# One activation table set, work moved to GpSimd, a table of due times and reordered transposes in a gated linear attention with two expert layers

## The chip, the cores and the metric

The kernel runs on one core of a Trainium2 chip. The metric is the device time of one execution in microseconds; of several executions the median is given. The profile is one profiled execution, and its times count from the span's start.

## The reference

A gated linear attention over 4 batches, 8 heads, 768 steps and a head size of 48 feeds two dense layers on 3072 tokens. All data are float32.

```python
f = 1.0 / (1.0 + np.exp(-f_logit))
for t in range(S):
    state = f[:, :, t, :, None] * state + np.einsum('bhd,bhe->bhde', k[:, :, t], v[:, :, t])
    y[:, :, t] = np.einsum('bhd,bhde->bhe', q[:, :, t], state)
# y -> x: 3072 tokens x 384
h = x @ w_in                                   # 384 x 2048
g = np.where(h >= 1, h, np.where(h <= -1, 0, (h + 1) ** 2 / 4))
x = g @ w_out                                  # 2048 x 384
gate = x @ w_gate; val = x @ w_val             # 384 x 1536 each
out = (gate / (1 + np.exp(-gate)) * val) @ w_out2   # 1536 x 384
```

The gates' logits are scaled by eight after they are drawn.

## The kernel before

**Tiles.** The attention is cut into 24 units: unit u holds 128 steps of batch u % 4, all heads, in two chunks c of 64 steps. The layers run over six groups of 512 tokens; a group is four units. A pass is one layer over one group; `PASSES` orders the twelve: first layer groups 0 and 1, second layer 0 and 1, and so on. The first layer needs the output of the group's four units, so units 0 to 3 come ahead of everything and units 4 to 7 during pass 0; units 8 to 23 are worked in two groups of eight, during the second layer's passes.

**A unit.** ScalarE and VectorE make the running products of the gates and their inverses (tiles e, x). For units 0 to 3 that is done with logarithms: `log_ops` (L496 to L503) takes exp, VectorE a minimum, ScalarE ln; a matmul sums (`at_cum`, tile psc), and two exponentials follow (L520, L526). For the others `decay_ops` (L532) takes exp and sigmoid, VectorE adds one (L548, L553) and scans (L559, L567). VectorE multiplies k (L574) and q (L584). TensorE makes the scores (psa, L606), transposes k (pst, L614), updates the state (psu, L670) and makes the output (psy, L699). ScalarE copies pst to kn. The mask is VectorE's (L632) or, for units from 4 on, ScalarE's copy and GpSimd's select. `at_state` adds psu to the state (L680) and multiplies it by the chunk's decay (L682), both on VectorE; `at_state_out` (L690) copies the state on GpSimd into vs or vf, which psy reads. In `at_burst` a visit of units 8 to 23 is made of up to three parts: psu of one unit, psa and pst of the next, and psy of the one before, which is an operation of its own.

**Precision.** An expert product is three matmuls: the high part of a float32 number times the high part, and the two cross terms. `c_b`, `c_sh`, `c_or`, `c_sg`, `c_h`, `c_l` make the weights' two parts from 64-bit input, each pair of blocks once; pairs go to DRAM and are loaded from there in later passes. `g_hi` and `g_lo` (L802, tile gl, the remainder) split what lies between two products.

**Zeroing.** Parts of vs, vf and y and the scans' tables d1 and dr must hold constants; they are written at L317 to L331, L475, L476 and L713.

**Order.** A planner writes the order of all engines' work. Every operation is added with an engine, a duration, its dependencies, a due time (`prio`) and buffers that it takes and gives; the planner steps through them, and among those of an engine that can start soon takes the one that is due first. So each engine's queue, SP's queue of DMA issues among them, has an order fixed at build time. An operation with a `tab` other than the last one costs 1.28 us in the plan. While TensorE would wait, ahead of the first expert products, the planner puts in filler matmuls (tile wt, L839), the planned gap divided by `FQ` in number.

## Time and profile before

| what | us |
|---|---|
| median of 3 runs | 958.18 (957.96 to 959.22) |
| profiled execution | 956.27 |
| its span | 954.5 |
| TensorE (matmul) busy | 935.5 |
| VectorE busy | 544.8 |
| ScalarE busy | 466.6 |
| GpSimd busy | 153.7 |

PE is TensorE, PEld its weight loads, DVE VectorE, ACT ScalarE, POOL GpSimd, and SP the engine that issues DMAs. L-numbers are lines of the kernel before. A stage table gives the engines in the order PE, PEld, DVE, ACT, POOL, and where one line is asked for, that line's engine alone. An engine counts as busy from the start of an instruction to its end. TensorE's instructions overlap, so its busy time is not a measure of its pace.

### The profile page before, as it was taken

How to read it: one execution, taken by the hardware profiler on the slowest of the kernel's cores; microseconds unless marked ns; L12 is line 12 of the kernel's file. 1: busy time of each engine (PE TensorE's matmuls, PEld its weight loads, DVE VectorE, ACT ScalarE, POOL GpSimd, SP SyncE). 2: the span in 40 equal slices, each digit the busy share in tenths (PEclk: the TensorE clock that was granted, in tenths of full speed). 3: DMA queues.
4: the chain of work that ended last, by engine and by line, in shares of the span. 5: the costliest groups of instructions: out<-in, count | busy, mean ns of one | idle time of the engine just before them, and what ended most of it. 6: DMA issues, size and time to landing. Idle time of an engine off the chain costs nothing.

```text
span 954.5 us, 15762 instructions
## 1 busy us (share of the span) xinstructions
PE 935.5 (98%) x6312; PEld 763.6 (80%) x6312; DVE 544.8 (57%) x794; ACT 466.6 (49%) x728; POOL 153.7 (16%) x256
## 2 busy tenths in 40 slices
PE   7899999999999999999999999999999999999996
PEld 7766778888888888888888888888888888888884
DVE  6999988998976565333435645664433433433332
ACT  6867766644445446545444425464654543222221
POOL 6435702113122131000000002132000000000000
PEclk9999999999999999999999999999999999999998
DMA  7936789688736872106647005576101755001001
GB/s 293 272 101 202 219 288 388 227 312 302 287 104 223 275 223 60 51 0 231 199 166 210 1 28 180 195 264 205 48 3 65 277 190 196 1 1 34 1 0 38
DMA packets 50594, 151.66 MB, mean 159 GB/s; under 512 B 5424, under 2 KB 24624, under 8 KB 50512
## 3 DMA queue, kind: packets, MB, share of 16 engines
q1 hardware_dynamic: 50512, 150.56, 46.9%
q8 instruction: 52, 0.85, 0.4%
q14 instruction: 30, 0.25, 0.1%
HBM read 110.43 MB, written 36.18 MB: 154 GB/s over the span
## 4 chain that ended last, share of the span: by engine, by line
PE 90%; DVE 3%; ACT 3%; DMA 1%; issue 1%; POOL 1%; DVEq 0%; POOLq 0%; ACTq 0%; SPq 0%
PE hp L773 19%; PE gps L773 15%; PE vps L773 15%; PE acc L425 11%; PE acc L426 11%; PE acc L427 11%; PE psy L699 2%; PE wt L839 1%; DMA raw<-w 1%; PE pst L614 1%; PE acc L811 1%; DVE raw L378 1%; DVE w L410 1%; PE psb L670 1%; PE psb L607 1%
## 5 line engine op out<-in xcount | busy, mean ns | idle before, releaser
L773 PE MATMUL hp<-xh,w 128*128 128x512 f32 x576 | 194.9, 395 | 0.3 <-DVE g L785 0.3
L425 PE MATMUL acc<-gh,w 128*128 128x512 f32 x480 | 187.2, 390 | 0.0
L426 PE MATMUL acc<-gl,w 128*128 128x512 f32 x480 | 187.0, 390 | 0.0
L427 PE MATMUL acc<-gh,w 128*128 128x512 f32 x480 | 186.8, 389 | 0.0
L773 PE MATMUL gps<-xh,w 128*128 128x512 f32 x432 | 146.5, 393 | 0.2 <-DVE sg L793 0.2
L773 PE MATMUL vps<-xh,w 128*128 128x512 f32 x432 | 144.7, 389 | 0.0
L773 PEld LDWEIGHTS hp<-xh,w 128*128 128x128 f32 x576 | 108.0, 188 | 24.5 <-issue 1.7
L785 DVE SCALAR_TENSOR_TENSOR g<-g,hp 128x512 f32<-128x512 f32 x96 | 65.7, 684 | 98.9 <-ACT g L782 98.7
L778 ACT ACTIVATE g<-hp,half 128x512 f32<-128x512 f32 x96 | 66.2, 690 | 100.6 <-PE hp L773 95.8
L773 PE MATMUL hp<-xl,w 128*128 128x512 f32 x288 | 112.0, 390 | 0.3 <-DVE xl L433 0.3
L793 DVE TENSOR_TENSOR sg<-gps,sg 128x512 f32<-128x512 f32 x72 | 49.6, 689 | 104.5 <-ACT sg L789 104.3
L797 ACT CAST gh<-sg 128x512 fp32r<-128x512 f32 x72 | 44.7, 621 | 130.2 <-DVE sg L793 130.2
L426 PEld LDWEIGHTS acc<-gl,w 128*128 128x128 f32 x480 | 90.1, 188 | 19.3 <-DVE gl L802 0.7
L425 PEld LDWEIGHTS acc<-gh,w 128*128 128x128 f32 x480 | 90.1, 188 | 18.8
L427 PEld LDWEIGHTS acc<-gh,w 128*128 128x128 f32 x480 | 90.1, 188 | 18.7
L789 ACT ACTIVATE sg<-gps 128x512 f32<-128x512 f32 x72 | 43.1, 599 | 113.7 <-PE gps L773 108.1
L773 PEld LDWEIGHTS gps<-xh,w 128*128 128x128 f32 x432 | 81.1, 188 | 17.9 <-DVE sg L793 0.7
L773 PEld LDWEIGHTS vps<-xh,w 128*128 128x128 f32 x432 | 81.1, 188 | 16.8
L802 DVE TENSOR_TENSOR gl<-g,gh 128x512 fp32r<-128x512 f32 x88 | 62.0, 704 | 47.0 <-ACT gh L797 46.8
L773 PE MATMUL gps<-xl,w 128*128 128x512 f32 x216 | 84.2, 390 | 0.0
L773 PE MATMUL vps<-xl,w 128*128 128x512 f32 x216 | 84.0, 389 | 0.0
L797 ACT CAST gh<-g 128x512 fp32r<-128x512 f32 x88 | 54.6, 620 | 57.2 <-DVE g L785 57.0
(146 smaller groups left out, 1281.3 us busy)
## 6 DMA issues: line engine op xcount, KB each, us to landing
w<-w2d SPq DMA_DIRECT2D x36, 768.0 KB, 4.3
raw<-w SPq DMA_DIRECT2D x34, 768.0 KB, 7.1
w<-w1d SPq DMA_DIRECT2D x32, 768.0 KB, 6.0
w2d<-w SPq DMA_DIRECT2D x18, 768.0 KB, 8.4
w1d<-w SPq DMA_DIRECT2D x16, 768.0 KB, 7.7
qk<-qk SPq DMA_DIRECT2D x20, 448.0 KB, 7.5
x2d<-o SPq DMA_DIRECT2D x18, 256.0 KB, 2.4
xl<-x2d SPq DMA_DIRECT2D x6, 768.0 KB, 7.9
```

Of the source, the lines that this page charges most:

```text
L378: nc.vector.scalar_tensor_tensor(out=lo, in0=hi, scalar=3, in1=lo, op0=ALU.logical_shift_left, op1=ALU.bitwise_or)
L425: nc.tensor.matmul(o, w[:, 0, wsl], xh, start=first, stop=False)
L426: nc.tensor.matmul(o, w[:, 0, wsl], xl, start=False, stop=False)
L427: nc.tensor.matmul(o, w[:, 1, wsl], xh, start=False, stop=last)
L699: nc.tensor.matmul(psy[0:48, i], vs[0:112, 0, c, p], a["ma"][0:112, i], start=True, stop=True)
L773: nc.tensor.matmul(hp, w[:, p, k * 128:(k + 1) * 128], x[:, k], start=i == 0, stop=i == len(steps) - 1)
L778: nc.scalar.activation(g, hp, AF.Relu, bias=half, scale=0.5)
L785: nc.vector.scalar_tensor_tensor(out=g, in0=g, scalar=1.0, in1=hp, op0=ALU.min, op1=ALU.max)
L789: nc.scalar.activation(sg, gps, AF.Sigmoid)
L793: nc.vector.tensor_tensor(out=sg, in0=p, in1=sg, op=ALU.mult)
L797: nc.scalar.copy(gh, g)
L802: (nc.gpsimd if pool else nc.vector).tensor_tensor(out=gl, in0=g, in1=gh.bitcast(F32), op=ALU.subtract)
```

## The change

- ScalarE loads one table set by name ahead of all; in the planner exp and ln are one `tab`, and the exponentials of units 2 and 3 no longer wait for those of unit 1.
- The zeroing of vf and of y for unit 2 is GpSimd's; d1 and dr are filled by an operation of their own on VectorE, on which the scans depend.
- For units 0 to 7 (`PST`) the multiplication by the decay becomes a planner operation on GpSimd, save the first chunk of units 0 to 3.
- For units 4 and 6 (`ADACT`) ScalarE adds the one. In pass 0 GpSimd makes the remainders of blocks 8, 10, 12 and 14 (`POOL_G`).
- In a visit psy is part of the burst and comes ahead of pst.
- `DUE` replaces the due times of 487 operations: those of units 0 to 7 with their loads (indices up to 201), the preparation of the first layer's weights (535 to 654), and pass 0 with the start of pass 1 (867 to 1044).
- Fillers: `FQ` is 0.125 instead of 0.12, and they may use a second buffer when the first is taken.
- Some durations and latencies in the planner's entries are new; the diff shows those of exp, minimum and ln, and leaves out those of loads.

```diff
--- before.py
+++ after.py
@@ -35,7 +35,7 @@
 POOL_K = ()
-POOL_G = 0
+POOL_G = (8, 10, 12, 14)
 SEL = (4, 5, 6, 7)
@@ -46,11 +46,75 @@
 EARLY2 = (3, 5, 7, 9, 11)
-FT, FQ, F0 = 60, 0.12, 4
+FT, FQ, F0 = 60, 0.125, 4
 KK = DM // 128
 BLEAD, BGAP = 34.0, 14.0
+ADACT = (4, 6)
+PST = (0, 1, 2, 3, 4, 5, 6, 7)
+DUE = {
+    0: 16.29, 1: -0.01, 2: -73.18, 3: -11.59, 4: 27.73, 5: -265.18, 6: -156.68, 7: -253.62, 8: -166.14, 9:
...
+}
 EXTRA = {0: 13.0, 2: 4.0}
@@ -75,7 +139,7 @@
         after, left, ready = {}, {}, {}
-        free, done, tab = dict(Pool=5.0, DVE=2.5), {}, None
+        free, done, tab = dict(Pool=5.0, DVE=1.8), {}, None
         for i, o in enumerate(ops):
@@ -125,13 +189,13 @@
             del ready[o["eng"]][i]
-            idle = min(self.slots["py"], default=t) <= free.get("PE", 0.0) + 0.3
+            idle = next((k for k in ("py", "pa") if min(self.slots[k], default=t) <= free.get("PE", 0.0) + 0.3), None)
             for tag in o["take"]:
             if fill and o["eng"] == "PE" and t < FT and idle:
-                fill(int((t - max(free.get("PE", 0.0), F0)) / FQ))
+                fill(int((t - max(free.get("PE", 0.0), F0)) / FQ), idle)
             o["t"] = t
@@ -291,6 +355,7 @@
+    nc.scalar.preload_act_table_set("natural_log_exp_and_others")
     x2d = dram.tile([128, KK, NT], F32, name="x2d")
@@ -314,10 +379,6 @@
     nc.gpsimd.memset(uno, 1.0)
-    nc.vector.memset(d1, 0.0)
-    nc.vector.memset(d1[:, :, 0:1], 1.0)
-    nc.vector.memset(dr, RCAP)
-    nc.vector.memset(dr[:, :, 0:1], 1.0)
     nc.vector.memset(half, 0.5)
@@ -472,8 +533,8 @@
             VF[2 + i] = t[:, i]
-            nc.vector.memset(t[0:64, i, 1], 0.0)
-            nc.vector.memset(t[64:112, i, 0], 0.0)
+            nc.gpsimd.memset(t[0:64, i, 1], 0.0)
+            nc.gpsimd.memset(t[64:112, i, 0], 0.0)
@@ -545,12 +606,12 @@
                 lambda: nc.scalar.activation(x, x, AF.Exp, scale=-1.0),
-                lambda: nc.vector.tensor_scalar(x, x, 1.0, None, op0=ALU.add),
+                lambda: nc.scalar.activation(x, x, AF.Copy, bias=1.0) if u in ADACT else nc.vector.tensor_scalar(x, x, 1.0, None, op0=ALU.add),
             ]
             lambda: nc.scalar.activation(x, x, AF.Sigmoid),
-            lambda: nc.vector.tensor_scalar(e, e, 1.0, None, op0=ALU.add),
+            lambda: nc.scalar.activation(e, e, AF.Copy, bias=1.0) if u in ADACT else nc.vector.tensor_scalar(e, e, 1.0, None, op0=ALU.add),
         ]
@@ -650,7 +711,7 @@
-    def at_burst(a, s):
+    def at_burst(a, s, y=None):
@@ -658,6 +719,9 @@
             at_psa(a, [t[:, 0:4 * C].rearrange("p (a t) -> p a t", a=4) for t in both])
+        if y:
+            at_pe3(y)
+        if a:
             at_pst(a, "h", 2)
@@ -673,13 +737,16 @@
         b = u % B
-        src = ST[b]
         if u < B and c == 0:
-            src = a["psu"][c]
-        else:
-            nc.vector.tensor_tensor(out=ST[b], in0=a["psu"][c], in1=ST[b], op=ALU.add)
-        pend = a["pp"].rearrange("p (a c) t -> p a c t", c=2)[:, :, c, C - 1:C]
-        nc.vector.tensor_tensor(out=ST[b], in0=src, in1=pend.to_broadcast([112, NP, D]), op=ALU.mult)
+            at_pend(u, c, a["psu"][c], nc.vector)
+            return
+        nc.vector.tensor_tensor(out=ST[b], in0=a["psu"][c], in1=ST[b], op=ALU.add)
+        if u not in PST:
+            at_pend(u, c, ST[b], nc.vector)
+
+    def at_pend(u, c, src, eng):
+        pend = A[u]["pp"].rearrange("p (a c) t -> p a c t", c=2)[:, :, c, C - 1:C]
+        eng.tensor_tensor(out=ST[u % B], in0=src, in1=pend.to_broadcast([112, NP, D]), op=ALU.mult)
@@ -700,6 +767,12 @@
+    def at_d():
+        nc.vector.memset(d1, 0.0)
+        nc.vector.memset(d1[:, :, 0:1], 1.0)
+        nc.vector.memset(dr, RCAP)
+        nc.vector.memset(dr[:, :, 0:1], 1.0)
+
     def at_y(u):
@@ -710,7 +783,7 @@
         if u < 4:
-            nc.vector.memset(a["y"][32:64], 0.0)
+            (nc.gpsimd if u else nc.vector).memset(a["y"][32:64], 0.0)
...
@@ -888,7 +961,7 @@
             if not odd:
-                E["y", u] = add("DVE", 1.1, lambda u=u: at_y(u), (), -44.8 + u, ("w" if u else "y",))
+                E["y", u] = add("Pool" if u else "DVE", 0.95, lambda u=u: at_y(u), (), -44.8 + u, ("w" if u else "y",))
             yc = E["yc", u] = add("ACT", 1.18, lambda u=u: at_yc(u), (p3, E["y", u // 2 * 2]), b + 4, (), ("py",))
@@ -927,11 +1000,8 @@
         pb = py = None
-        if a or c:
-            dur = 0.2 + 0.9 * (a is not None) + 0.52 * (c is not None)
-            pb = add("PE", dur, lambda: at_burst(a, c), deps, b + 1, take, give)
-        if y:
-            py = add("PE", 1.05, lambda: at_pe3(y), (pb,) if pb else deps, b + 1 - 9 * (pb is not None), () if pb else take, ("mab",))
+        dur = 0.2 + 0.9 * (a is not None) + 0.52 * (c is not None) + 0.95 * (y is not None)
+        pb = py = add("PE", dur, lambda: at_burst(a, c, y), deps, b + 1, take, give + (("mab",) if y else ()))
         mc = None
@@ -949,21 +1019,22 @@
+    E["d"] = add("DVE", 1.1, at_d, (), -20.0)
     for u in range(NU):
...
             )
...
         if u == 2:
-            E["vf"] = add("DVE", 1.7, at_vf, (), -44.5, ("w",))
+            E["vf"] = add("Pool", 1.7, at_vf, (), -44.5, ("w",))
         before = {2: E.get("vf"), 3: E.get("vf"), 4: E.get(("p3", 0)), 5: E.get(("p3", 1))}.get(u, E.get(("p3", u - 2)))
         if u < 4:
...
             E["lv", u] = add("Pool", 1.4, lambda u=u: at_copyv(u), (E["n", u], before), b + 1)
@@ -978,9 +1049,9 @@
                     bl = at_base(u // 4 * 4) - 6 + u % 4 + (i or 0)
-                    ex = add("ACT", 0.9 * h, lambda lg=lg: lg(0), (E["lx", u],) + ((E["ep", 1],) if u == 2 else ()), bl, tab="exp")
-                    mn = add("DVE", 0.9 * h, lambda lg=lg: lg(1), (ex,), bl)
-                    ln = add("ACT", 0.9 * h, lambda lg=lg: lg(2), (mn,), bl + 4, tab="ln")
+                    ex = add("ACT", 1.02 * h, lambda lg=lg: lg(0), (E["lx", u],), bl, tab="exp")
+                    mn = add("DVE", 0.75 * h, lambda lg=lg: lg(1), (ex,), bl)
+                    ln = add("ACT", 1.15 * h, lambda lg=lg: lg(2), (mn,), bl + 0.4, tab="exp")
                     for h in (0, 1) if i is None else (i,):
@@ -997,7 +1068,7 @@
                 ex, sg = sg, ex
-            ad = add("DVE", 0.72, lambda F=F: F[None][2](), (ex,), b - 2)
+            ad = add("ACT" if u in ADACT else "DVE", 1.07 if u in ADACT else 0.72, lambda F=F: F[None][2](), (ex,), b - 2)
             for i in range(2):
@@ -1005,8 +1076,8 @@
         else:
-            R = add("DVE", 1.3, lambda u=u: at_scan_r(u), (E["ad", u],), b)
-            Pp = add("DVE", 1.28, lambda u=u: at_scan_p(u), (E["sg", u],), b + 0.2)
+            R = add("DVE", 1.3, lambda u=u: at_scan_r(u), (E["ad", u], E["d"]), b)
+            Pp = add("DVE", 1.28, lambda u=u: at_scan_p(u), (E["sg", u], E["d"]), b + 0.2)
         pk = u in POOL_K
...
@@ -1041,9 +1112,14 @@
             leave(u - 1, p2)
-        s0 = add("DVE", 0.37 if u < B else 0.75, lambda u=u: at_state(u, 0), (p2, so0, E.get(("st", u - B))), b + 2.2, (), ("at",))
+        pm = u in PST
+        s0 = add("DVE", 0.37 if u < B or pm else 0.75, lambda u=u: at_state(u, 0), (p2, so0, E.get(("st", u - B))), b + 2.2, (), ("at",))
+        if pm and u >= B:
+            s0 = add("Pool", 0.7, lambda u=u: at_pend(u, 0, ST[u % B], nc.gpsimd), (s0,), b + 2.2)
         so1 = add("ACT" if u in ACT_S else "Pool", 0.72 if u in ACT_S else 0.8 if u < 4 else 1.4, lambda u=u: at_state_out(u, 1), (s0, E.get(("p3", u - 2 if u > 5 else u - 4)), E.get("vf") if u in (2, 3) else None), b + 2.2)
-        s1 = add("DVE", 0.75, lambda u=u: at_state(u, 1), (so1, E.get(("st", u - 1)) if odd else None), b + 4, (), ("at", two) if odd else ("at",))
+        s1 = add("DVE", 0.37 if pm else 0.75, lambda u=u: at_state(u, 1), (so1, E.get(("st", u - 1)) if odd else None), b + 4, (), ("at",) if pm else ("at", two) if odd else ("at",))
+        if pm:
+            s1 = add("Pool", 0.7, lambda u=u: at_pend(u, 1, ST[u % B], nc.gpsimd), (s1, E.get(("st", u - 1)) if odd else None), b + 4, (), (two,) if odd else ())
         E["st", u] = s1
...
@@ -1153,8 +1229,7 @@
                 hi = None if nat else add("ACT", 0.65, keep(("gh", key), g_hi, ("g", key)), (mx,), b + 1, ("gh",))
-                pool = s == 1 and pool_n < POOL_G and j % 2 == 0
-                pool_n += s == 1
+                pool = n == 0 and j in POOL_G
                 lo = None if nat else add(
@@ -1200,6 +1275,8 @@
         o["order"] = tuple(d for d in (takeX.get(d[1] - 1) if isinstance(d, tuple) else d for d in o["order"]) if d is not None)
+    for i, p in DUE.items():
+        P.ops[i]["prio"] = p
     with tc.manual_schedule():
```

## Rows read from the trace of the kernel before

**Rows 1.** Stage table: stretch, us, busy us per engine (instructions), granted clock, DMA, GB/s.

```profile
0.00:42.95 42.95, 35.32 (x638) 32.26 (x638) 32.53 (x68) 34.63 (x49) 23.51 (x61) 0.96 0.82 278
42.95:126.72 83.77, 81.53 (x673) 56.90 (x672) 78.49 (x107) 59.92 (x95) 43.82 (x49) 1.00 0.58 183
126.72:954.50 827.78, 818.67 (x5003) 674.41 (x5003) 433.82 (x621) 372.04 (x586) 86.42 (x146) 1.00 0.44 150
```

**Rows 2.** ScalarE in order of time: start, us, instructions, [idle before, its releaser].

```profile
3.50 1.11 ACT L500 ACTIVATE x<-x 128x448 f32<-128x448 f32 x2 [1.40 <-DMA x<-xn]
6.39 1.28 ACT L502 ACT_TABLE_LOAD   x1 [1.78 <-DVE x L501]
...
10.23 0.60 ACT L520 ACTIVATE e<-psc 112x512 f32<-112x512 f32 x1
```

**Rows 3.** The chain that ended last, from 0 to 140 us: start, duration, what.

```profile
19.66 1.28 ACT L520
...
47.33 1.54 PE wt L839 x24
...
125.71 0.96 DVE xl L433
```

**Rows 4.** VectorE in order of time, the same columns as ScalarE's.

```profile
4.02 0.38 DVE L475 MEMSET vf<- 64x384 f32 x1
...
5.92 0.69 DVE L501 TENSOR_SCALAR x<-x 128x448 f32<-128x448 f32 x2
...
10.86 0.69 DVE L574 TENSOR_TENSOR qk<-qk,e 112x512 f32<-112x512 f32 x1 [3.07 <-ACT e L520]
```

**Rows 5.** All engines in order of time, ahead of the first expert matmul.

```profile
40.00 3.02 PE L839 MATMUL wt<-btri 128*64 128x64 f32 x38
...
41.31 0.55 DVE L750 TENSOR_TENSOR xl<-px,xh 128x384 fp32r<-128x384 f32 x1
```

**Rows 6.** GpSimd in order of time.

```profile
5.12 0.41 POOL L331 MEMSET vs<- 48x384 f32 x1
9.32 1.53 POOL L489 COPY vs<-qk 64x192 f32<-64x192 f32 x4 [3.79 <-DMA qk<-vv]
```

**Rows 7.** DMA issues of SP in order of time: start, time to issue.

```profile
1.73 0.91 SPq L456 DMA_DIRECT2D qk<-qf  x2
```

**Rows 8.** The DMA issued from 1.2 to 1.9 us: KB, us to landing.

```profile
qk<-qf SPq DMA_DIRECT2D x1, 512.0 KB, 5.7
```

**Rows 9.** Line L682 alone in the first pass, stage table.

```profile
43.00:127.00 84.00, 4.58 (x8) 1.00 0.58 184
```

**Rows 10.** Groups from 43 to 127 us: count, busy us, mean ns, idle before.

```profile
L404 POOL CAST w<-raw 128x768 fp32r<-128x768 f32 (+1 forms) x13 | 13.7, 1051 | 17.6 <-DVE raw L391 14.1 <-issue 3.3
...
L690 POOL COPY vs<-st 48x192 f32<-48x192 f32 x12 | 10.5, 872 | 4.4 <-DVE st L682 3.9
...
L802 DVE TENSOR_TENSOR gl<-g,gh 128x512 fp32r<-128x512 f32 x7 | 5.3, 762 | 0.0
...
L591 POOL COPY mb<-ma 64x512 f32<-64x512 f32 x4 | 4.9, 1224 | 6.9 <-DVE ma L584 6.9
```

**Rows 11.** TensorE's waits: for whom, total us, times, longest.

```profile
PE psy L699 <- POOL vs L690: 1.0, 1, 1.0
```

**Rows 12.** Single lines: count, duration in ns min/median/max, first and last start.

```profile
L682 DVE TENSOR_TENSOR st<-st,x x40: 357/359/818, 19.0 to 673.6; 112x192 f32<-112x192 f32 x40
...
L690 POOL COPY vs<-st x84: 337/344/2087, 17.9 to 672.9; 48x192 f32<-48x192 f32 x84
```

**Rows 13.** VectorE in order of time, late in the first pass.

```profile
117.02 1.55 DVE L682 TENSOR_TENSOR st<-st,e 112x192 f32<-112x192 f32 x1
```

**Rows 14.** The chain behind visits of attention, in two stretches.

```profile
270.98 2.09 PE gps L773 x9
...
307.15 2.27 PE gps L773 x9
```

More of the change, by code (lines that the diff above doesn't have):

```diff
@@ L833, in x2_load, with fill @@
         nc.sync.dma_start(out=getX(n)[1].bitcast(F32), in_=x2d[:, :, g * 512:(g + 1) * 512])
-    def fill(n):
-        t = ps.tile([64, 64], F32, tag="acc0", name="wt")
+    def fill(n, where):
+        t = ps.tile([64, 64], F32, tag="acc0" if where == "py" else "acc1", name="wt")
         for _ in range(n):
@@ L957, in fast_path @@
             E["lx", i] = add(
-                "SP", 1.6, lambda i=i: at_loadx(i), (), b - 12 if i >= NLOG else -51.65 if i else -52.0, ("x",), (), 2.0,
+                "SP", 1.6 if i >= NLOG else 1.15, lambda i=i: at_loadx(i), (), b - 12 if i >= NLOG else -51.85 if i else -52.0, ("x",), (), 3.0 if i >= NLOG else 3.5 if i else 2.6,
                 (E.get(("l", i - 1)) if i != 2 else E["l", 0],),
             )
-        E["l", u] = add("SP", 1.75 if u < 4 else 2.1, lambda u=u: at_load(u), (), b - 11.9 if u >= 4 else -51.9 + 0.05 * u + 0.3 * (u > 1), ("w",) if u < 4 else ("qk", "vn"), (), 2.0, (E["lx", u // 2 * 2] if u != 2 else None, E.get(("l", u - 1))))
+        E["l", u] = add("SP", 2.5 if u == 0 else 1.4 if u < 4 else 2.1, lambda u=u: at_load(u), (), b - 11.9 if u >= 4 else -51.9 + 0.05 * u + 0.3 * (u > 1), ("w",) if u < 4 else ("qk", "vn"), (), 3.5 if u < 4 else 3.0, (E["lx", u // 2 * 2] if u != 2 else None, E.get(("l", u - 1))))
         if u == 2:
-            E["vf"] = add("DVE", 1.7, at_vf, (), -44.5, ("w",))
+            E["vf"] = add("Pool", 1.7, at_vf, (), -44.5, ("w",))
         before = {2: E.get("vf"), 3: E.get("vf"), 4: E.get(("p3", 0)), 5: E.get(("p3", 1))}.get(u, E.get(("p3", u - 2)))
         if u < 4:
-            E["n", u] = add("SP", 0.65, lambda u=u: at_loadn(u), (), -51.7 + 0.2 * u + 0.1 * (u > 1), (), (), 2.0, (E["l", u], E.get(("n", u - 1))))
+            E["n", u] = add("SP", 0.5, lambda u=u: at_loadn(u), (), -51.7 + 0.2 * u + 0.1 * (u > 1), (), (), 3.5, (E["l", u], E.get(("n", u - 1))))
             E["lv", u] = add("Pool", 1.4, lambda u=u: at_copyv(u), (E["n", u], before), b + 1)
@@ L1030, in fast_path @@
         if u in SEL:
-            mc = add("ACT", 1.5, lambda u=u: at_mcopy(u), (pa, qc), b + 2.4, (), ("at",) * 2 if u >= 4 else ())
+            mc = add("ACT", 1.5, lambda u=u: at_mcopy(u), (pa, qc), b + 2.4, (), ("at",) * 2 if u >= 4 else ("pa",))
             mask = add("Pool", 2.6, lambda u=u: at_msel(u), (mc,), b + 2.5)
@@ L1077, in fast_path @@
             p = use - 16
-            last_d = dma = add("SP", 2.6, lambda jb=jb: c_dma(jb), (), p - 8, (slot,), (), 2.2, (last_d,))
+            last_d = dma = add("SP", 1.95 if r == 0 and i < 4 else 2.6, lambda jb=jb: c_dma(jb), (), p - 8, (slot,), (), 3.3, (last_d,))
             cg = dma
@@ L1102, in keep @@
         return go
-    oms, pool_n, lin_at = [], 0, None
+    oms, lin_at = [], None
     for r, ns in enumerate(runs):
```

59 rows, old and new, of the table DUE are left out of this document.

## Prediction

> **What bounds the kernel now.** I read the stage table first [rows 1]. From 126.72 us to the end TensorE is busy 818.67 of 827.78 us, and what is missing there is the tail; the change can take time from that stage only by shortening TensorE's own work. The first 42.95 us hold no expert matmul at all: they are the attention of units 0 to 3, and no engine is full in them (ScalarE 34.63, VectorE 32.53, GpSimd 23.51 us busy). Between them lies the first expert pass: TensorE counts as busy for 81.53 of 83.77 us, but VectorE for 78.49, so two engines are close to the limit together, and GpSimd stands at 43.82, about half. So three stages, three questions: how much sooner can the first matmul start, can VectorE and GpSimd then keep up, and what does a visit of attention cost TensorE later on.
>
> For the front I read each engine's own order, then the chain. On ScalarE a load of a function table (1.28 us) stands ahead of each change between exp and ln: one at 6.39 ahead of the first ln, another ahead of the exp at 10.23 [rows 2]. There are four such loads before the first expert matmul, the first at 6.39, the last at 19.66, which stands itself on the chain [rows 3]. The one at 6.39 came that late because VectorE took the minimum between exp and ln only at 5.92, behind four zeroing instructions of 0.38 us from 4.02 on, though the first exponentials ran from 3.50 [rows 2, 4]. At the end of the front, xl of unit 3 is written from 41.31 on for 0.55 us, while TensorE runs 38 filler matmuls from 40.00 to the first real one at 42.95 [rows 5].
>
> **The change part by part: the front.** (a) Zeroing moved. The four vf instructions (4 x 0.38 = 1.5 us) and y of unit 2 go to GpSimd, and d1 and dr are filled later. GpSimd writes such zeros in 0.41 us and then sits idle for 3.79 us until a load lands, at 9.32 [rows 6]; the moved work is 4 x 0.41 and one y (0.95 in the planner's entry), 2.6 us in all, and lies in that gap. Were the gap gone, the copies of v would come up to 2.6 us later. VectorE can then take the minimum as soon as the first of two exponentials is done, at about 4.1 instead of 5.92: 1.8 us.
> (b) One table set. The loads at 6.39 and ahead of 10.23 go: 2 x 1.28 = 2.6 us. With (a) the exponentials of units 0 and 1 could begin 4.4 us sooner, at 5.8. But they multiply q and k, and q and k of unit 0 are issued at 1.73 and land 5.7 us later, at 7.4 [rows 7, 8]; that first multiplication stood at 10.86 [rows 4]. So the gain here is 10.86 - 7.4 = 3.4 us, and the remaining microsecond waits for memory. The other two loads (ahead of the ln of units 2 and 3, and the one at 19.66) are worth 2 x 1.28 = 2.6 us more, and the second is on the chain [rows 3]. Sum 6.0 us. The Trainium skill, "ScalarE: Activation LUTs", section "What ACT_TABLE_LOAD costs", adds a drain to the load and has a switch at 2.66 us; the rows show no drain, and by the page an estimate for four switches would be 10.6 us instead of 5.1, and the time some 5 us lower.
> (c) Fillers. TensorE could have started when xl was there, 41.86, and started at 42.95: 1.1 us [rows 5]. The divisor goes from 0.12 to 0.125, 4% fewer fillers, but filling is now also allowed where it was not; I take 0.5 us.
> (d) The due times set new priorities for the operations of units 0 to 7, of the first weights, of the first pass and of the start of the second, on all five queues, SP's loads included. They change no duration, and the trace before can't show them. Bounds: ScalarE is idle for 42.95 - 34.63 = 8.3 us of the front [rows 1], of which the first 3.50 can't go, nor all of the waits for transfers and for TensorE, so at most some 3 us; in the other direction an operation set ahead of its data blocks its queue, and the longest such wait for a load in these rows is 3.79 us [rows 6]. I take 0, between the two.
> Front: 6.0 + 0.5 = 6.5 us sooner, from 3 (little more than the step that memory bounds survives) to 9.5.
>
> **The first pass.** VectorE loses the decay multiplications of units 4 to 7, 8 in 4.58 us [rows 9]; four remainders gl, 4 x 0.76 = 3.05 [rows 10]; the additions for units 4 and 6, 0.72 each in the planner's entry. Together 9.0 us. It gains d1 and dr, 4 zeroing instructions, 1.1 us in the planner's entry. But if the front is 6.5 us shorter, the weight work that VectorE did in those 6.5 us, 6 us at its share there, has to be done later. Net it has 9.0 - 1.1 - 6 = 1.9 us less: enough to keep up, no more. What could be gained are TensorE's visible waits: 1.54 us of fillers at 47.33 [rows 3] and 1.0 us for GpSimd's state copies [rows 11]; the second pass then starts behind xl at 125.71 [rows 3]. I take 1.0 us of these 2.5.
> GpSimd gets those 8 multiplications, 4 more of units 0 to 3, and the four remainders. No row has an operation of it with two inputs. From below: its copy of 192 columns alone, 0.34 us [rows 12], and for a remainder what VectorE takes, 0.76; from above: the same copy among VectorE's work in this stage, 0.87, and one of 512 columns, 1.22 [rows 10]. So 12 x 0.34 + 4 x 0.76 = 7.1 us to 12 x 0.87 + 4 x 1.22 = 15.3 us; I take 11, nearer to the crowded rows, since this stage is crowded. GpSimd goes to 55 of 84 us. Behind each moved operation wait the casts of weights, 13 in 13.7 us [rows 10], and behind those VectorE's subtraction and the matmul. The two additions on ScalarE (1.07 us each in the planner's entry) lie in its idle time, 83.77 - 59.92 us [rows 1]; without that they are 2.1 us.
> That sum takes VectorE's time as freed. The long forms speak against it: the multiplication takes 0.36 us alone [rows 12], 4.58 / 8 = 0.57 here, and 1.55 once at 117.02 [rows 13]. The Trainium skill, "SBUF — State Buffer", section "SBUF: two separate sides", has a cause: GpSimd and VectorE hold one port pair in turn, for whole instructions. By that rule moved work goes on blocking VectorE; the long row agrees, without naming the cause.
> First pass: -1.0 us, from -2.5 to +5 (about half of GpSimd's 11 us blocks VectorE).
>
> **Transposes last.** In a visit of units 8 to 23 with all three parts the order was psu and psa, pst, psy. The first expert block behind psy took 2.27 us on the chain (at 307.15), the one behind pst 2.09 (at 270.98) [rows 14]. Merged, psy comes earlier and pst last: 0.18 us in each of 12 such visits (six in each group of eight units), 2.2 us. The copy kn now waits for psy as well, and ScalarE's queue behind it; units come 14 us apart by the planner, so I cost that at nothing; if it showed, the whole 2.2 would be gone. TensorE has no gap there, so this is on the path in full.
>
> **Sum.** -6.5 - 1.0 - 2.2 = -9.7 us on the profiled execution's 956.27 (span 954.5): 946.6. That execution is 1.9 us below the median of the runs shown, so 948.5 for a median. Ends of the bounds: -9.5 - 2.5 - 2.2 = -14.2 gives 944.0; -3 + 5 + 0 = +2 gives 960.2.
>
> **Rivals.** *Given back in the first pass.* The front is 6.5 us shorter, but VectorE, near full, can't do its weight work sooner, since the moved operations block it: +5 instead of -1. 958.18 - 6.5 + 5 - 2.2 = 954.5. For it speak the 78.49 of 83.77 us and the row of 1.55; against it the net 1.9 us less work.
> *Everything fits.* All of the front's bound, no wait left in the pass: 944.0. For it: no engine is full in the front. Against: units 2 and 3 wait for their own loads.
> *The set isn't shared.* If loads still stand between exp and ln, only (a), (c), the pass and the visits are left: -1.8 - 0.5 - 1.0 - 2.2 = -5.5, so 952.7. The Trainium skill, "ScalarE: Activation LUTs", section "Table sets: the hidden batching unit", lists one set with both functions; no row here shows it.
> *Slower: GpSimd's queue.* The place is the states of units 0 to 7. Each multiplication now stands between VectorE's sum and GpSimd's own copy, behind casts. If each of the 12, with its wait, comes as late as the longest form (1.55 us) and TensorE waits for it as it did for GpSimd once, that is 12 x (1.55 - 0.36) = 14.3 us: 958.18 - 6.5 - 2.2 + 14.3 = 963.8. It decides from (6.5 + 2.2) / 12 = 0.7 us of delay per multiplication. For it: TensorE's wait of 1.0 [rows 11]. Against: only the first of a unit's two lies between its psu and its psy, and nobody waits for those of units 0 to 3 before unit 4.
>
> **How the numbers follow.** Forecast 0.57, everything fits 0.14, given back 0.15, set not shared 0.05, slower 0.09. A measurement of this kernel tells 0.2%, 1.9 us, from no change, so the limits are 956.3 and 960.1. Faster: 0.57 + 0.14 + 0.05 and two thirds of given back, 0.86; the same: the rest of that one, 0.05; slower 0.09. The range takes in the bounds but for the slower case and the outer tenth of either side: 943.5 to 957.5.
>
> **What would show it.** In the profile of the changed kernel: no table load on ScalarE between the first exp and the first sigmoid; the minimum at about 4.2 us; k of unit 0 multiplied at about 7.5; the first expert matmul at 36 to 37; the second pass about 83 us behind it; psy ahead of pst, and an expert block of 2.09 us behind pst; from there the same pace to the end. I am wrong if the first matmul starts later than 40, or if the first pass grows by over 4 us with longer waits for GpSimd or for weights.

## The result: 9.7 us faster, 948.3 against 958.0 us

The changed kernel takes 948.28 us (median of 5 runs, 947.45 to 949.00), the kernel before 957.96 on the same chip; the ratio is 0.9901, with an interval from 0.9889 to 0.9912. The forecast was 948.5. The total came out; the places did not, and the rest of this document is about that.

The profiled execution of the changed kernel took 949.00 us, span 947.1, 0.7 above its median, as that of before was 1.7 below its own. From profile to profile only 7.4 us are gained. Where they lie is read off the times at which the same expert matmul starts in both traces:

| expert matmul | before, us | after, us | gained |
|---|---|---|---|
| first | 42.95 | 42.51 | 0.44 |
| 101st | 78.75 | 77.01 | 1.73 |
| 301st | 138.91 | 135.09 | 3.82 |
| 1501st | 434.71 | 429.78 | 4.93 |
| last (3648th) | 945.23 | 939.28 | 5.94 |
| end of span | 954.5 | 947.1 | 7.4 |

So the front brought 0.4 us (forecast 6.5), the first pass 3.4 (forecast 1.0), the visits 2.1 (forecast 2.2), and 1.4 lie behind the last matmul, where the output leaves. The same three output transfers end that piece in every kernel of this document; from the last matmul's start to the end of the span it takes 9.2 us before and 8.7 in set_alone, below, and 7.2 to 7.9 in all others, and why is not shown.

The stage table of the kernel after (stretch, us, busy us and instructions of each engine, granted clock, DMA share, GB/s) answers to [rows 1]; passes two and on now start by 117:

```profile
0.00:42.51 42.51, 37.01 (x647) 33.44 (x647) 32.54 (x59) 30.26 (x45) 32.09 (x70) 1.00 0.90 310
42.51:117.00 74.49, 73.59 (x623) 50.47 (x622) 71.06 (x89) 57.04 (x90) 56.35 (x58) 1.00 0.55 167
```

GpSimd's busy time rises to 32 and 56 us. VectorE is no less full than before, though its work was lightened: 71.06 of 74.49 us. The second row covers 9 us less than that of before, but not the same matmuls: 264 expert matmuls start ahead of 117 us here, and 248 started ahead of 126.72 before. The table above counts matmuls and so compares like with like.

ScalarE and VectorE at the start, after (start, us, instruction, [idle before, its releaser]), against [rows 2] and [rows 4]:

```profile
3.46 1.13 ACT L561 ACTIVATE x<-x 128x448 f32<-128x448 f32 x2 [1.35 <-DMA x<-xn]
4.95 1.23 ACT L563 ACTIVATE x<-x,uno 128x448 f32<-128x448 f32 x2 [0.36 <-DVE x L562]
7.77 0.60 ACT L581 ACTIVATE e<-psc 112x512 f32<-112x512 f32 x1 [1.60 <-PE psc L571]
```
```profile
4.17 1.28 DVE L562 TENSOR_SCALAR x<-x 128x448 f32<-128x448 f32 x2
8.40 0.70 DVE L635 TENSOR_TENSOR qk<-qk,e 112x512 f32<-112x512 f32 x1 [2.95 <-ACT e L581]
```

The table loads are gone, the minimum starts at 4.17 instead of 5.92, and k of unit 0 is multiplied at 8.40 instead of 10.86. These 2.5 us are real, and yet the first expert matmul gained 0.4. TensorE in the same stretch shows the first leak (psc are the cumulative sums of units 0 and 1, wt the fillers, psa the first products of unit 0):

```profile
5.72 3.73 PE L571 MATMUL psc<-btri,x 128*112 128x128 f32 x16 [0.59 <-POOL vs L392]
9.37 2.59 PE L912 MATMUL wt<-btri 128*64 128x64 f32 x26
11.89 0.27 PE L667 MATMUL psa<-ma,qk 48*64 48x64 f32 x1
```

The 16 psc take 3.73 us, where before took 1.97; behind them stand 26 fillers in the same queue, and psa starts at 11.89, 2.0 us after VectorE has written its operand (9.85). Before, psa started at 12.37. The slow psc are the clock's: the trace's clock record begins with the rise to the upper of TensorE's two levels (1.2 and 2.4 GHz), at 11.29 us here and at 7.20 before, and the views print 1.00 ahead of that first record too. The fillers show the same moment, in the rows of tile wt (stretch, us, busy us and number, clock, DMA): 18 of them fall in 1.90 us ahead of it, 10 in 0.50 us behind it.

```profile
9.40:11.30 1.90, 1.90 (x18) 1.00 1.04 418
11.40:11.90 0.50, 0.50 (x10) 1.00 1.07 439
```

Before, psc started at 8.46, behind the rise; the change starts them at 5.72, and the fillers and psc from 2.09 us on then ran at the lower level. The second leak is GpSimd's copies of the states at the end of the front:

```profile
27.72 2.08 POOL L757 COPY vf<-st 48x192 f32<-48x192 f32 x2 [1.49 <-DVE st L749]
...
33.44 3.15 POOL L757 COPY vf<-st 48x192 f32<-48x192 f32 x2 [3.08 <-DVE st L749]
```

Two copies that take 0.34 us each alone [rows 12] last 2.08 and 3.15 us, while VectorE works on weights; psy of units 2 and 3 waits for them. The experiments ask what these leaks are worth, and which parts of the change earned the 9.7 us.

### The profile page after: what moved, and what is told of

It is laid out like the page before. It is cut to its first block, busy times and chain, and to the rows that moved or that the text cites. A ratio compares the mean times of both kernels' runs of the same rounds, so it can differ in the third digit from the quotient of the medians.

```text
span 947.1 us, 15701 instructions
## 1 busy us (share of the span) xinstructions
PE 933.1 (99%) x6296; PEld 762.7 (81%) x6296; DVE 543.0 (57%) x771; ACT 462.0 (49%) x726; POOL 181.8 (19%) x277
## 4 chain that ended last, share of the span: by engine, by line
PE 88%; DVE 5%; POOL 2%; DMA 2%; issue 2%; ACT 1%; POOLq 0%; DVEq 0%; ACTq 0%; SPq 0%
PE hp L846 18%; PE vps L846 15%; PE gps L846 15%; PE acc L487 11%; PE acc L488 11%; PE acc L486 11%; PE psy L766 2%; DMA raw<-w 1%; PE pst L675 1%; DVE raw L439 1%; PE wt L912 1%; DVE w L471 1%; PE psb L734 1%; PE psb L668 1%; PE psc L571 1%
## 5 line engine op out<-in xcount | busy, mean ns | idle before, releaser
L875 DVE TENSOR_TENSOR gl<-g,gh 128x512 fp32r<-128x512 f32 x84 | 59.0, 703 | 50.5 <-ACT gh L870 50.5
```

The lines of the kernel that those rows point to most:

```text
L875: (nc.gpsimd if pool else nc.vector).tensor_tensor(out=gl, in0=g, in1=gh.bitcast(F32), op=ALU.subtract)
```

## The experiments

All times in this table are of one kernel each; "rise" is when the clock rose to its upper level, "psc" is what the first 16 psc took, "psa" and "first" are the starts of the first psa and of the first expert matmul, "301st" the gain on the kernel before at the 301st expert matmul, all from the profiled execution.

| kernel | median, us | ratio to before (interval) | rise | psc | psa | first | 301st |
|---|---|---|---|---|---|---|---|
| before | 957.96 | 1 | 7.20 | 1.97 | 12.37 | 42.95 | 0 |
| after | 948.28 | 0.9901 (0.9889, 0.9912) | 11.29 | 3.73 | 11.89 | 42.51 | -3.82 |
| no_set | 949.52 | 0.9919 (0.9906, 0.9933) | 10.66 | 3.73 | 12.31 | 43.95 | -2.38 |
| no_due | 952.09 | 0.9943 (0.9930, 0.9957) | 10.81 | 3.73 | 11.67 | 42.60 | -1.76 |
| old_visit | 949.37 | 0.9913 (0.9898, 0.9928) | 10.45 | 3.73 | 11.51 | 42.12 | -4.49 |
| work_on_dve | 945.58 | 0.9878 (0.9863, 0.9893) | 9.29 | 3.71 | 11.02 | 40.96 | -6.67 |
| mult_on_dve | 945.30 | 0.9877 (0.9859, 0.9896) | 10.14 | 3.73 | 11.37 | 41.30 | -6.20 |
| copy_on_act | 947.85 | 0.9902 (0.9884, 0.9919) | 5.26 | 1.97 | 9.28 | 39.81 | -6.06 |
| both | 945.30 | 0.9873 (0.9853, 0.9893) | 10.47 | 3.73 | 11.52 | 40.81 | -5.89 |
| set_alone | 958.28 | 1.0006 (0.9994, 1.0019) | 7.27 | 2.02 | 10.90 | 44.39 | +2.92 |
| no_gap | 948.12 | 0.9903 (0.9887, 0.9920) | 5.20 | 1.97 | 8.83 | 41.11 | -5.54 |
| no_fill | 949.38 | 0.9917 (0.9900, 0.9933) | 9.54 | 3.73 | 9.91 | 41.32 | -2.80 |
| mult_no_gap | 946.53 | 0.9887 (0.9871, 0.9904) | 4.94 | 1.97 | 8.83 | 40.93 | -5.63 |
| less_weights | 944.62 | 0.9868 (0.9848, 0.9889) | 10.48 | 3.73 | 9.93 | 40.10 | -7.31 |

Each ratio is to before on the same chip, where it took 957.3 to 958.0 us. Intervals are some 1.1 to 2 us either way, so two kernels less than 2 us apart are told apart only with the help of their traces. The rise differs ahead of any edited instruction, so part of a difference in psa, first and 301st is its doing; copy_on_act, no_gap and mult_no_gap, with rises at 4.94 to 5.26 us, are best compared with each other. In no_fill, which has no fillers, the clock fell and rose again several times; the table has the first rise.

### The table set

no_set is the changed kernel without

```
-    nc.scalar.preload_act_table_set("natural_log_exp_and_others")
```

> The changed kernel without the named table set, all orders as they are, so four table loads of 1.28 us come back on ScalarE ahead of the first expert matmul. Theory A (what the prediction said): ScalarE's loads are on the path of the front, so it loses 2.6 to 6 us against the changed kernel: 951 to 954 us. Theory B (the front of the changed kernel is set by the state copies on GpSimd, its chain holds 6.9% of the first 46 us for them and hardly any of ScalarE): the loads lie beside other work and the time rises by under 1 us, to at most 949.3.

Its ratio is 0.0018 higher, 1.7 us. Against the changed kernel's trace it is 1.44 us later at the first expert matmul, 1.45 at the 301st and 0.99 at the last. Four loads of 1.28 us, 5.1 us together, are therefore worth 1.0 to 1.7 us: between the two theories, nearer to the one in which something else is late next. set_alone puts the set (and nothing else, but for the planner's name for the logarithm's table) into the kernel before:

```
+    nc.scalar.preload_act_table_set("natural_log_exp_and_others")
-                    ln = ... bl + 4, tab="ln")
+                    ln = ... bl + 4, tab="exp")
```

> The kernel before with the named table set, and its logarithm costed under the same set as its exponential; nothing else of the change. Theory by the prediction's order: exponential, minimum and logarithm of the first units come as in the changed kernel, k of unit 0 at about 7.5 to 8.5 instead of 10.86 and y of unit 0 about 2.5 us sooner, but the end of the front follows by no more than 0.5 to 1.7 us, as leaving the set out of the changed kernel cost 1.4 at the first expert matmul: 956.0 to 957.5. Rival: here, without due times fitted to the later order, the early units' work is not hidden behind other queues and the set brings its whole 2.6 to 6.0 us: 951.5 to 955.

Nothing is gained: 1.0006, and neither theory held. With the logarithm's table named otherwise the planner also writes another order, so this is not the set by itself. The first steps came sooner as in the changed kernel (psa at 10.90, psy of unit 0 at 17.84 instead of 19.51), but the first expert matmul starts at 44.39, 1.4 later. ScalarE's rows name what took over, set_alone (first fence) and before (second):

```profile
34.59 0.48 ACT L747 CAST xh<-px 128x384 fp32r<-128x384 f32 x1
35.09 1.28 ACT L553 ACT_TABLE_LOAD   x1
36.38 1.07 ACT L553 ACTIVATE x<-x 112x1040 f32<-112x1040 f32 x1
37.36 0.56 ACT L721 COPY y<-psy 48x512 f32<-48x512 f32 x1
```
```profile
34.94 0.48 ACT L746 CAST xh<-px 128x384 fp32r<-128x384 f32 x1
35.31 1.07 ACT L551 ACTIVATE e<-x 112x1040 f32<-112x1040 f32 x1
36.29 0.57 ACT L720 COPY y<-psy 48x512 f32<-48x512 f32 x1
...
40.60 1.28 ACT L552 ACT_TABLE_LOAD   x1
```

At xh of unit 2 only 0.35 us of the lead is left. Then the sigmoid of unit 4, with a table load of its own, stands ahead of unit 3's copies of y, which start at 37.36, 1.07 later than before; in before that load came at 40.60, behind them. The clock was at its lower level from 37.99 to 44.82 us here and from 37.92 to 41.34 in before, and xh of unit 3 is 1.42 later. So the time saved went to a later unit's work, which the new order put ahead. A part that is worth over 1 us inside the change is worth nothing in the order that the planner writes around it alone.

### The due times

no_due leaves the table of due times unapplied:

```
-    for i, p in DUE.items():
-        P.ops[i]["prio"] = p
```

> The changed kernel without the table of due times: every operation has the due time of its formula again, all else as changed. Theory A (the moved work and the table set make the gain, the order is worth nothing, as I had put it): 947 to 950 us. Theory B (the order of the first 120 us is what shortens the first pass): it loses the 3.4 us that the first pass gained, or more, 951.5 to 957 us.

952.09 us, ratio 0.0042 higher: the due times are worth 4.0 us, as the second theory said. They do nothing for the front (42.60 against 42.51). 2.1 us are lost by the 301st matmul and 2.5 later. TensorE's waits in no_due (for whom, total us, times, longest): the 2.3 us for sg lie behind 130 us and are most of the later part, the 1.9 for psy lie in the front, and the 1.2 for g lie in the first pass, as do the fillers of the second fence:

```profile
PE gps L846 <- DVE sg L866: 2.3, 2, 1.2
PE psy L766 <- issue: 1.9, 1, 1.9
PE hp L846 <- DVE g L858: 1.2, 1, 1.2
```
```profile
46.91 1.03 PE L912 MATMUL wt<-btri 128*64 128x64 f32 x14
```

In the changed kernel TensorE waits 0.2 us for sg behind 130 us, and there is no filler behind the first expert matmul: the 1.54 us of [rows 3] are gone.

### The transposes

old_visit puts pst ahead of psy again:

```
+        if a:
+            at_pst(a, "h", 2)
         if y:
             at_pe3(y)
-        if a:
-            at_pst(a, "h", 2)
```

> The changed kernel with pst ahead of psy in a visit, as before. The 12 visits of three parts should cost 0.17 to 0.18 us more each: 950.2 to 950.5 us against 948.3, and nothing in the first 130 us should move. If the waiting copy kn had cost something in the new order, the loss would be smaller than 1 us.

949.37 us, under the 950.2 to 950.5 expected. Its front was 0.4 us sooner with the same order there, and its clock rose 0.84 sooner; from the 301st matmul to the last it gains nothing on the kernel before (-4.49, -4.47), where the changed kernel goes from -3.82 to -5.94, 2.1 us. Matmul by matmul, the changed kernel draws ahead at twelve blocks behind visits, by 0.16 to 0.17 each, 2.0 together, and old_visit at none; the rest is 0.5 that before lost near its 598th matmul against all kernels here, set_alone included, less 0.44 that after lost near its 832nd. By the ratios it is 1.1, within their intervals. In the chain of waits the expert block behind a visit takes 2.10 us after (first fence, behind pst) and 2.27 in old_visit (second fence, behind psy), as in [rows 14]:

```profile
281.46 0.53 PE pst L675 x4
281.99 2.10 PE gps L846 x9
```
```profile
281.46 2.27 PE gps L846 x9
```

### The work moved to GpSimd

work_on_dve issues the twelve decay multiplications of units 0 to 7 and the four remainders on VectorE, at the same places; mult_on_dve only the multiplications:

```
-  lambda u=u: at_pend(u, 0, ST[u % B], nc.gpsimd)
+  lambda u=u: at_pend(u, 0, ST[u % B], nc.vector)
   (the same for the second one; in work_on_dve also g_lo)
```

> The changed kernel with the 12 decay multiplications and the four remainders issued on VectorE, at the same place in the order; zeroing stays on GpSimd. Theory A (relieving VectorE shortens the first pass): VectorE has some 7 us more to do before the second pass and the first pass grows by 2 to 4 us, 950 to 952 us. Theory B (the two engines block each other, so moved work frees nothing): within 1 us of the changed kernel, 947.3 to 949.3 us, with VectorE's mean durations lower than in the changed kernel.

> The changed kernel with only the twelve decay multiplications of units 0 to 7 back on VectorE; the four remainders stay on GpSimd. Theory multiplications: these cost the 2 to 3 us, since each takes 0.51 to 2.36 us on GpSimd against 0.36 to 0.69 on VectorE and a state copy of the same engine is queued behind it: 945.3 to 946.5, first expert matmul near 41.0. Theory remainders: the remainders hold it in the passes, and the multiplications gave VectorE room: 947.5 to 949, though the first expert matmul may come at 41 to 42.

945.58 and 945.30 us: this part of the change costs 2.2 (by the ratios) to 3.0 us (by the medians), all of it the multiplications, as their theory said. In work_on_dve neither theory held: one saw a loss of 2 to 4 us in undoing the move, the other no difference. The size is less sure than the sign. no_gap and mult_no_gap, below, differ by the multiplications alone too and are 1.5 to 1.6 us apart; in their traces, whose clocks rose at 5.20 and 4.94, it is 0.17 us at the first expert matmul and 0.30 at the last. The rows of the multiplication, after (first fence) and in mult_on_dve (count, ns min/median/max, first and last start):

```profile
L749 POOL TENSOR_TENSOR st<-st,x x8: 507/962/2364, 18.3 to 81.1; 112x192 f32<-112x192 f32 x8
...
L749 POOL TENSOR_TENSOR st<-st,e x4: 507/512/2291, 93.5 to 111.6; 112x192 f32<-112x192 f32 x4
```
```profile
L749 DVE TENSOR_TENSOR st<-st,x x40: 327/364/685, 17.4 to 668.3; 112x192 f32<-112x192 f32 x40
```

On GpSimd it takes 0.51 us at least and up to 2.36, the twelve 13.3 us together; on VectorE it takes 0.33 to 0.69. GpSimd's queue in the front, after (first fence) and in mult_on_dve (second), shows what stands behind it:

```profile
18.29 1.06 POOL L749 TENSOR_TENSOR st<-st,x 112x192 f32<-112x192 f32 x1
19.29 1.07 POOL L652 COPY mb<-ma 64x512 f32<-64x512 f32 x1
...
22.12 1.53 POOL L757 COPY vs<-st 48x192 f32<-48x192 f32 x4
```
```profile
17.74 0.62 POOL L652 COPY mb<-ma 64x512 f32<-64x512 f32 x1
...
20.94 0.73 POOL L757 COPY vs<-st 48x192 f32<-48x192 f32 x2
```

The next copies of states start 1.18 us later, 0.52 of it because psa was that much later. mult_on_dve and the kernel named both, below, have the lowest medians of the whole kernels (945.30), 3.0 us below the change, 2.3 to 2.7 by the ratios.

### The state copies

copy_on_act is the changed kernel, and both is work_on_dve, with the state copies of units 2 and 3 on ScalarE:

```
-            if u in ACT_S:
+            if u in (2, 3):
                 nc.scalar.copy(to, ST[b][r])
```

> The changed kernel with the eight state copies of units 2 and 3 (48x192, line 757) issued on ScalarE instead of GpSimd, at the same place. Theory GpSimd held: in the changed kernel the pair of unit 2 spans 2.08 us and that of unit 3 3.15 us, while a single such copy takes as little as 0.34; VectorE runs 128x768 operations on two SBUF operands beside them, and every psy waits for the pair. On ScalarE the pair of unit 3 starts in an idle stretch and should take some 0.7 to 1.0, so the first expert matmul comes 1.5 to 3.0 us sooner (at 39.5 to 41.0), and the time falls to 945.0 to 947.0. Theory weights: the front's end is set by ScalarE's and VectorE's weight work, all of which has to be done by then anyway; the copies are merely beside it, ScalarE's own queue grows by 2 to 3 us, and the first expert matmul stays at 42.0 to 43.0 with 948 to 949.5.

> The same copies on ScalarE, and the decay multiplications of units 0 to 7 and the remainders on VectorE. Theory GpSimd held: the gains add, since the one lies at 16 to 26 us and in the passes and the other at 26 to 37 us: 1.5 to 3.0 below the 945.58 of the kernel with multiplications and remainders on VectorE alone, so 942.5 to 944.1, first expert matmul at 38.0 to 39.5. Theory weights: no sooner than that kernel, 945 to 947, first expert matmul at 40.5 to 41.5.

The copies shrink as expected: 0.73 us for the two of unit 3, where GpSimd took 3.15. In copy_on_act the first expert matmul comes 2.70 us sooner, as the first theory wanted, but not for its reason:

```profile
5.71 1.97 PE L571 MATMUL psc<-btri,x 128*112 128x128 f32 x16 [0.59 <-POOL vs L392]
7.62 1.73 PE L912 MATMUL wt<-btri 128*64 128x64 f32 x26
9.28 0.27 PE L667 MATMUL psa<-ma,qk 48*64 48x64 f32 x1
...
32.48 0.73 ACT L755 COPY vf<-st 48x192 f32<-48x192 f32 x2
```

The same 16 psc, from the same start, took 1.97 instead of 3.73 us in this execution, whose clock rose at 5.26, and psa was 2.61 us sooner long before any edited instruction. The median says so too: 947.85, no better than the change. Beside no_gap, below, whose clock rose at 5.20 and whose psy of unit 0 starts at the same 15.0 us, the copies bring the first expert matmul 1.3 us, and the last none (937.35 and 937.31). In both, whose psc were slow, the first expert matmul gains 0.15 on work_on_dve, 0.65 if one counts that its psa was 0.5 later, and the time is the same within the intervals (945.30 against 945.58), as the theory of weights had it. Of the 1.5 to 3.0 us expected at the first matmul 0.2 to 1.3 were to be had, and none at the end: the held copies alone don't set the front's end.

### The fillers

no_gap leaves out the 26 fillers between psc and the first psa, mult_no_gap does the same to mult_on_dve, and no_fill has no fillers at all (FT = 0):

```
     def fill(n, where):
+        fills[0] += n > 0
+        if fills[0] == 2:
+            return
```

> The changed kernel without the fillers (26 matmuls in the trace) that stand between the cumulative sums psc of units 0 and 1 and the first psa, and nothing else. In the changed kernel's profile these 26 take 2.52 us (9.37 to 11.89), and the 16 psc before them 0.228 us each where later ones take 0.121; the data of psa were there at 9.85. Theory TensorE's own queue: the front's gain was lost there, psa of unit 0 starts at 9.9 to 10.1 instead of 11.89, and the first expert matmul comes 1.0 to 2.0 us sooner, at 40.5 to 41.5; the time falls by 1 to 2, to 946.3 to 947.3. Theory fillers raise the clock: without them the matmuls of units 0 and 1 go on at the slower rate (0.22 us and more for a psc of unit 2), and what is saved is lost: first expert matmul at 42 to 43.5, 948 to 950. Theory later chain: ScalarE's and GpSimd's work at 26 to 38 us sets the end in any case, and the first expert matmul stays within 0.4 of 42.5.

> The changed kernel with the twelve multiplications on VectorE and without the fillers ahead of the first psa. Theory TensorE's own queue: the two add, 1 to 2 us below the 945.30 with the multiplications alone: 943.3 to 944.3, first expert matmul at 39.3 to 40.3. Theories clock and later chain: 945 to 947, first expert matmul at 41 to 42.5.

> The changed kernel without any filler matmul. Theory TensorE's own queue: as without the fillers ahead of the first psa, and the last 28 fillers that end 0.5 us behind xl go too: first expert matmul at 40.0 to 41.0, 945.8 to 947. Theory fillers raise the clock: psc, px and the first expert matmuls run at the slower rate, a psc takes 0.22 us or more in units 2 and 3 and an hp matmul 0.43 instead of 0.23 for a while; the first expert matmul at 43 to 46, the first pass longer by 2 to 4, 951 to 956.

no_gap starts psa at 8.83, 3.1 us sooner, with quick psc again; the first expert matmul is 1.4 us sooner in that execution, and the median the same as the change's (948.12). In mult_no_gap psa is 2.5 us sooner than in mult_on_dve, the first expert matmul 0.4, and the time 1.2 us longer, which the intervals don't separate. Most of what TensorE's queue loses early thus costs nothing later: of the three theories "later chain" comes nearest, though not within its 0.4 us in the execution with quick psc. The psc stand ahead of the fillers left out, so they were not quick because of the edit. Without any filler the granted clock falls, as rows of no_fill show (first fence; after, second fence, has 1.00):

```profile
12.00:20.00 8.00, 7.34 (x125) 0.79 1.03 414
20.00:30.00 10.00, 8.54 (x247) 1.00 0.99 314
30.00:41.32 11.32, 6.36 (x74) 0.80 0.90 286
41.32:50.00 8.68, 8.68 (x23) 0.67 0.32 91
```
```profile
30.00:42.51 12.51, 10.76 (x193) 1.00 0.92 273
42.51:50.00 7.49, 7.27 (x28) 1.00 0.34 91
```

Its first expert matmul comes 1.2 us sooner than after's, but the first 18 take 6.89 us instead of 4.59, and at the 301st it is 1.0 us behind the change. The fillers cost the front about a microsecond and return more than that. no_fill's 949.38 us lies between its two theories.

### Is it the weight work?

From 30 to 41 us VectorE is busy 10.65 of 11 us in mult_no_gap. less_weights takes from that kernel two steps in the conversion of the first six weight pieces, so that these weights come out wrong:

```
     def c_b(jb):
+        if len(cut) < 6:
+            cut.append(jb)
+            return
     def c_or(jb):
+        if any(jb is j for j in cut):
+            return
```

> The kernel with the multiplications on VectorE and without the fillers ahead of the first psa, with two steps of the conversion left out for the first six weight pieces (the scaling on ScalarE, line 425, and the joining of the bits on VectorE, line 439), so that these weights come out wrong; all else stands in the same order. Six times 0.935 us of ScalarE's and six times 0.96 of VectorE's time are gone, all but the last between 21 and 39 us. Theory full engines: ScalarE is busy 9.80 us of 20 to 30 us and VectorE 10.65 of 30 to 41, mostly with weights, and this sets the front's end, which is why sooner attention steps at 9 to 20 us bring so little; now the first expert matmul comes 2 to 4 us sooner than the 40.93 without this edit, at 37.0 to 39.0, and the time falls from 946.5 to 942.5 to 945. Theory chain: the attention's own steps one after the other (cumulative sum, copies of the states, psy, y, px) set it, and the weight work only fills the engines' waits: first expert matmul within 0.7 of 40.93, time 945 to 947.

Busy times of all engines in this stretch, mult_no_gap and less_weights, and less_weights' ScalarE and VectorE:

```profile
30.00:41.00 11.00, 9.38 (x135) 8.67 (x135) 10.65 (x16) 8.32 (x11) 7.96 (x7) 1.00 0.94 303
```
```profile
30.00:41.00 11.00, 10.19 (x151) 9.56 (x152) 6.82 (x12) 6.19 (x9) 5.57 (x8) 1.00 0.99 295
```
```profile
34.12 0.48 ACT L825 CAST xh<-px 128x384 fp32r<-128x384 f32 x1 [3.89 <-PE px L821]
```
```profile
31.21 0.36 DVE L755 TENSOR_TENSOR st<-psu,x 112x192 f32<-112x192 f32 x1 [1.53 <-PE psu L741]
```

VectorE falls to 6.82 us, ScalarE waits 3.89 us in one piece, and the first expert matmul is only 0.83 us sooner (at most 1.9, counting that slow psc had put psa 1.1 later), less than the 2 to 4 us of the theory of full engines and a little more than the 0.7 of the other. At the 301st matmul it is 1.7 us, and the time, 944.62, is 1.9 below mult_no_gap and in the range of full engines (942.5 to 945). So neither theory held as a whole: the weight work holds part of the front's end, and not all of it. New waits have come up: VectorE's 1.53 us for psu, and in the chain of waits fillers that end after what they fill for (30 of them until 36.79, where y was written by 36.47).

## Why the prediction came out, and where it failed

- **(a) Zeroing: right.** Minimum at 4.17, forecast 4.2; GpSimd's zeros lie in its idle stretch.
- **(b) One table set: the mechanism right, the worth wrong.** The loads are gone; "the set isn't shared" is out. k of unit 0 came at 8.40, not 7.5: it waited for e, and e 1.60 us for the slow psc, so memory was not the next limit. In copy_on_act, no_gap and mult_no_gap, whose clocks rose ahead of psc, it came at 7.48 as forecast, and there k of unit 1 waits 1.3 to 1.6 us for its load; the prediction moved psc ahead of the rise and left them as quick as before. The failed step is the sum "6.0": 3.4 and 2.6 us on ScalarE were booked in full at the first expert matmul. Measured: 1.0 to 1.7 us for the whole set inside the change, and nothing in set_alone's order. The prediction asked what is late next only at k, once, where it had to ask at every handover: by psa 0.5 us of the 2.5 was left. The clock explains only part: where psc were quick, the first expert matmul still came at 39.81 to 41.11, with a further edit each, 1.8 to 3.1 us sooner for the 6.5.
- **(c) Fillers: about right.** xl of unit 3 ends at 42.03 and the first expert matmul starts at 42.51: 0.5 us lost instead of 1.1. The clock, which the prediction left out, may be part of that: from 38 to 42 us 0.58 of it was granted before and 1.00 after. The fillers as such earn 1.5 us by the ratio of no_fill.
- **(d) Due times: the mis-sized term.** Taken as 0; measured 4.0 us, the largest part of the change. The bounds looked at the front alone, and the gain lies behind it, in the passes.
- **Front:** 0.44 for 6.5, outside its range of 3 to 9.5. The sign named for being wrong, a first matmul later than 40 us, came true.
- **First pass:** 3.4 for 1.0, outside the 2.5 taken as the most. The waits of [rows 3] and [rows 11] went (1.54 and 1.0), which the prediction had named. From the first to the 301st matmul it is 95.96 us before, 92.58 after and 94.55 in no_due, so the due times account for 2.0 of the 3.4; without them fillers of 1.03 us come back, and the wait for the state copies doesn't. VectorE's relief of the multiplications did none of it: with them back on VectorE that stretch is 91.41 (mult_on_dve), and 92.34 against 92.26 in mult_no_gap and no_gap. What did the other 1.4 is open.
- **Visits:** 2.0 at the twelve blocks themselves for 2.2, right with its mechanism.
- **Slower by GpSimd's queue:** did not win, but its mechanism is there. 1.5 to 3.0 us over 12 multiplications are 0.13 to 0.25 each, under the 0.7 from which it would have decided. GpSimd's share was mis-sized: 13.3 us for the multiplications and 5.8 for the remainders, 19.2 for the 11 taken and the 15.3 from above. That nobody waits for those of units 0 to 3 was wrong: GpSimd's next copies stand behind them.
- **Given back in the pass** and **everything fits** did not happen.

So 6.1 us too much in the front were made up by 2.4 in the pass, 1.4 behind the last matmul and 2.4 by which the profiled executions lie on opposite sides of their medians. The total was right by errors that cancelled.

**What stays open.** What sets the end of the front was not settled. Taking away TensorE's early fillers moved the first expert matmul by 0.4 us, the held copies by 0.2 to 1.3, and 5.6 us of weight work on each of two engines by 0.8 to 1.9; which work took over was traced in set_alone and less_weights alone. The parts' worths (due times 4.0, visits 2.0, set 1.0 to 1.7, multiplications -1.5 to -3.0) add up to some 5 of the 9.7 us; zeroing, additions on ScalarE and the output's end were not tried alone. Of each kernel one execution was traced, so how often the clock rises early, and what that does to the medians, is not shown.

## To carry to other kernels

Where several engines hand over to each other in a ramp, a saving on one is no saving at the end: follow it handover by handover to the first matmul that counts, and book only what is left there. A reordering that changes no duration is not worth zero for that; take it off alone, and it may prove the largest part. Before work is moved to the engine that looks idle, look at what of its own stands behind in the queue, and compare traces of two executions up to the first edited instruction before a difference is put down to the edit.

## What the runs showed of the hardware

- The same 16 matmuls at the same start took 3.73 us in some executions and 1.97 in others, a ratio of 1.9, near that of TensorE's two levels (1.2 and 2.4 GHz). The moment of the clock's rise decides it: in the ten kernels with the same TensorE instructions up to 5.7 us (fillers from 2.09 to 5.1, psc from 5.72) the clock record begins between 4.94 and 11.29 us, and only the three with a rise by 5.26 have quick psc. The Trainium skill, "TensorE: Matmul & The Clock Gate", section "Part 1: The HAM clock gate (the 'warmup' mystery)", says that the moment of the rise varies between runs of one kernel; these rows agree.
- Two copies of 48x192 took 3.15 us on GpSimd while VectorE ran operations with two inputs in SBUF, and 0.73 on ScalarE at the same place. The Trainium skill, "SBUF — State Buffer", section "SBUF: two separate sides", has the two engines hold a shared port pair in turn; the rows agree, without showing the cause.
- A switch of the function table is 1.28 us [rows 2], with no drain to be seen behind it in no_set either, and four of them were worth 1.0 to 1.7 us here. The 10.6 us estimated by the figure of the Trainium skill, "ScalarE: Activation LUTs", section "What ACT_TABLE_LOAD costs", are not borne out.
